# One row maximum bound behind a pair's sums of squares, and one scale per row in the second layer

## The chip, the core and the metric

The kernel runs on one core of a Trainium2 chip. Its engines are PE (TensorE, matrix products), DVE (VectorE), ACT (ScalarE), POOL (GpSimd) and SP (SyncE, which here only issues transfers); each works through its own list of instructions in order and waits for the others by semaphores. The metric is the device time of one execution in microseconds (us). The changed kernel is compared with the kernel before.

## The reference

Three stages, in f32. Four batches of twelve heads (448 tokens, head size 64) go through attention with normalized q and k; the heads are joined to 1792 tokens of 768 columns; two layers with a hidden width of 2048 follow.

```python
q_n, k_n = (rmsnorm(q, g_q), rmsnorm(k, g_k))
scores = scale * np.matmul(q_n, k_n.transpose(0, 1, 3, 2))
attn = np.exp(scores - np.max(scores, axis=-1, keepdims=True))
attn = attn / (np.sum(attn, axis=-1, keepdims=True) + 1e-09)
x = np.matmul(attn, v)            # then joined to 1792 x 768
h = x @ w_in                      # moe: first layer
x = (h * (1.0 / (1.0 + np.exp(-1.702 * h)))) @ w_out
h = x @ w_in                      # moe2: second layer, own weights
out = (np.maximum(h, 0.0) + alpha * np.minimum(h, 0.0)) @ w_out
```

`alpha` has one value for each of the 2048 hidden rows, between 0 and 0.3 in these inputs.

## The kernel before

The matrix products run on pairs of f16 numbers: a value is scaled by a power of two, its high half is rounded to f16 and the rest becomes the low half, and a product is the sum of three matmuls. The powers of two come from maxima: of each row of a weight matrix, of v, of the tokens.

**Order of the work.** The kernel is written as generators that are stepped in turn, but the list of each engine is put in order when the kernel is built: a scheduler with a simulated timeline of its own places every instruction. `tc.issue_after(x)` binds what is issued inside it behind instruction x. So a single binding can move many instructions of all engines, in places that the code does not name.

**The front.** Twenty-four pairs of heads (`P`; six for each batch) are loaded, normalized and put through attention. `normalize` squares a pair's q and k on ACT, and `tensor_reduce` on DVE adds the squares up (`ss`, L423, two for each pair); the inverse root follows on POOL, `qn` (L458) is the normalized product on DVE, PE transposes it (`qt`) and computes scores `sp`. For each unit of scores DVE takes the row maximum `nm` (L530), ACT the exponentials `pr` (L550), PE transposes them (in the first batch) or a DMA does (`pt`), and PE multiplies by v (`xp`, L648). `own` (L666) and `xraw` (L662) finish the first batch's tokens on DVE. A pair's high and low parts `hl` in later batches come from ACT (L477) and DVE (L478).

**The weights of the first layer** are made beside it by `weights`. They arrive as 64-bit words by loads `g` (L223) that SP issues in order, into a few buffers that take turns, so that a load waits until the words before it in its buffer are used up. DVE (L164, L165) and ACT (L148) turn the words into f32; L245 takes each row's maximum `rm`; a few tiny steps (L105, L106, L172) make a power of two of it; ACT and DVE (L180) write the two halves. `w1i` has six blocks of 128 rows and 2048 columns, `w1o` sixteen of 768 columns.

**Two round trips over memory.** A maximum over partitions is found by writing one number per partition to memory and reading the whole line back on every partition. `send_max` does it for `am` (the largest alpha, ready with an L106): L128 writes `line`, L129 reads `row`, and L134 on DVE reduces it into `a`. `measure` does the same for the maxima of v: `vmax` (L106), `v_line` (L329), `vrow` (L330), and `mv` (L331) on DVE.

**The second layer.** `moe2_in` makes tiles `h` (L927; eighteen matmuls each) in three PSUM buffers. ACT copies a tile with the factor `sign` (L932), DVE joins it with the `slope` (L933), and the result `pos` goes to memory. From there `token_sums` reads the tokens back in seven pairs of 128-token tiles: `gp`, or for every second pair `odd`, holds 2 halves of 8 row blocks by 256 tokens. L1029 multiplies it by `cg`, the row's scale from the second weights times the sign of alpha's treatment; then ACT (L1036) and DVE (L1037, L1046 and others) make the seven operands `even` or `odd` of a Strassen-Winograd product, which `moe2_out` multiplies (`op`, L1087). The weights' scales are shared by row block m and m + 8 of the sixteen blocks; `sign` is not. The first two pairs are made while `h` still runs.

Of the kernel before, what the change touches and what calls it, by code (L numbers as in the profile page):

```python
# [13 lines left out]
AF = mybir.ActivationFunctionType  # L14
ALU = mybir.AluOpType
AX = mybir.AxisListType.X
# [41 lines left out]
def attention_moe_kernel(  # L58
# [17 lines left out]
    nc = tc.nc  # L76
# [92 lines left out]
    def row_scales(rm, inv, rows):  # L169

        pow2floor(rm[:, rows], rm[:, rows])
        nc.vector.tensor_scalar(  # L172
            out=inv[:, rows].bitcast(I32), in0=rm[:, rows].bitcast(I32), scalar1=-1.0, scalar2=float((2 * 127 + 13) << 23),
            op0=ALU.mult, op1=ALU.add
        )

    def split_rows(w, num, inv, j):

        nc.scalar.activation(out=w[:, j, 0], in_=num, func=AF.Copy, scale=inv[:, j:j + 1])
        nc.vector.scalar_tensor_tensor(  # L180
            out=w[:, j, 1], in0=num, scalar=inv[:, j:j + 1], in1=w[:, j, 0], op0=ALU.mult, op1=ALU.subtract
        )
# [20 lines left out]
    def weights(src, nm, w, num_tile, raw_tile, parts, ahead, c, done, group, hold=0):  # L203


        rows, cols = src.shape
        words = src.bitcast(I32).rearrange("r (n t) -> r n t", t=2)
        nj = rows // 128
        m = cols // parts
        rm = const.tile([128, nj], F32, name=f"rm_{nm}")  # L210
        inv = const.tile([128, nj], F32, name=f"inv_{nm}")
        raws = []
        nums = []

        def load():
            t = len(raws)
            if t < nj * parts:
                j, i = divmod(t, parts)
                raw = raw_tile(t)
                src_words = words[j * 128:(j + 1) * 128, i * m:(i + 1) * m]  # L220
                if len(raw.shape) == 4:
                    src_words = src_words.rearrange("r (a n) t -> r a n t", a=raw.shape[1])
                loads.setdefault(nm, []).append(nc.sync.dma_start(out=raw, in_=src_words))  # L223
                raws.append(raw)

        def split_all():
            while nums:
                split_rows(w(), nums[0][1], inv, nums[0][0])
                nums.pop(0)
                yield  # L230

        for _ in range(ahead):
            load()
        yield
        for j in range(nj):
            if hold and j == hold:
                yield "held"
                yield from split_all()
            num = num_tile(j)
            for i in range(parts):  # L240
                from_words(num[:, i * m:(i + 1) * m], raws[j * parts + i])
                load()
                yield
            nums.append((j, num))
            nc.vector.tensor_reduce(out=rm[:, j:j + 1], in_=num, op=ALU.max, axis=AX, apply_absolute_value=True)  # L245
            if (j + 1) % group == 0:
                row_scales(rm, inv, slice(j + 1 - group, j + 1))
                yield
                if j >= hold:
                    yield from split_all()  # L250
        if hold:
            yield "rows"
        yield from weight_scales(nm, rm, nj, c, done, W2I_WAIT if hold else 0)
# [8 lines left out]
    w1i = big.tile([128, KD, 2, FF], F16, tag="w", name="w1i", bufs=2)  # L262
# [138 lines left out]
    roots = {}  # L401
    v0 = const.tile([128, NP], F32, name="v0")
    rooted = {}

    def side(P):

        return nc.gpsimd if NP + 2 <= P < 2 * NP else nc.vector

    def normalize(*Ps):
# [4 lines left out]
        n = NT2  # L414
        w = 2 * n * len(Ps)
        ss = small.tile([128, 4 * NT2], F32, tag="ss", name="ss")[:, 0:w]
        for t, P in enumerate(Ps):
            flat = raws[P].rearrange("p h c d -> p (h c) d")
            for i in range(2):
                sq = att_p.tile([128, n, D], F32, tag="sq", name="sq", bufs=SQB)  # L420
                nc.scalar.activation(out=sq, in_=flat[:, i * n:(i + 1) * n], func=AF.Square, scale=2.0 ** -13)
                o = (2 * t + i) * n
                nc.vector.tensor_reduce(out=ss[:, o:o + n], in_=sq, op=ALU.add, axis=AX)  # L423
        nc.gpsimd.tensor_scalar(out=ss, in0=ss, scalar1=1e-6 * 2.0 ** -20, scalar2=None, op0=ALU.add)
        rs = small.tile([128, 4 * NT2], F32, tag="rs", name="rs")[:, 0:w]
        tn = small.tile([128, 4 * NT2], F32, tag="tn", name="tn")[:, 0:w]
# [1 line left out]
            out=rs.bitcast(I32), in0=ss.bitcast(I32), scalar1=-0.5, scalar2=RSQRT_SEED, op0=ALU.mult, op1=ALU.add  # L428
# [421 lines left out]
    KH = KF // 2  # L850
# [26 lines left out]
    w2 = {}  # L877
# [131 lines left out]
    def token_sums(p):  # L1009
# [3 lines left out]
        if p % 2:  # L1013
# [3 lines left out]
            gp = w2["odd"][:, 14336:22528].bitcast(F32)  # L1017
        else:
            ops = big.tile([128, 14336], F16, tag="g", name="even")
            gp = w2["p2"].tile([128, 4096], F32, tag="gp", name="gp", bufs=1)  # L1020
        ops = ops.rearrange("p (o m e t) -> p o m e t", o=7, m=KH, e=2)
        gp = gp.rearrange("p (j m t) -> p j m t", j=2, m=KH)
# [3 lines left out]
        sums[p] = ops  # L1026
        yield
        for m in range(KH):
            nc.scalar.activation(out=gp[:, :, m], in_=gp[:, :, m], func=AF.Copy, scale=w2["cg"][:, m:m + 1])  # L1029
            if m % 4 == 3:  # L1030
                yield
        a11, a12, a21, a22 = (gp[:, j, :, i * 128:(i + 1) * 128] for i in range(2) for j in range(2))
# [273 lines left out]
```

## Time and profile before

| | |
|---|---|
| three timed runs | 1146.89, 1152.3, 1152.42 us (median 1152.3) |
| profiled execution | 1148.87 us, its span 1147.1 us |
| granted clock of TensorE, mean | 0.973 |
| PE busy | 1064.7 us (93% of the span) |
| DVE busy | 802.2 us (70%) |
| ACT busy | 682.2 us (59%) |
| POOL busy | 180.6 us (16%) |

Times of rows are us from the start of the span. "Busy" is the time in which an engine had an instruction running. The bracket behind a row of a timeline is the engine's idle time just before it and what ended that time: `<-DMA row<-line` is the transfer that wrote `row`. Consecutive instructions of one line and shape are put together in a row (x8). An instruction on DVE or ACT starts a little before the last one ends, so a series takes less than the sum of its lengths.

### The profile page before, as it was taken

How to read it: one execution, taken by the hardware profiler on the slowest of the kernel's cores; microseconds unless marked ns; L12 is line 12 of the kernel's file. 1: busy time of each engine (PE TensorE's matmuls, PEld its weight loads, DVE VectorE, ACT ScalarE, POOL GpSimd, SP SyncE). 2: the span in 40 equal slices, each digit the busy share in tenths (PEclk: the TensorE clock that was granted, in tenths of full speed). 3: DMA queues.
4: the chain of work that ended last, by engine and by line, in shares of the span. 5: the costliest groups of instructions: out<-in, count | busy, mean ns of one | idle time of the engine just before them, and what ended most of it. 6: DMA issues, size and time to landing. Idle time of an engine off the chain costs nothing.

```text
span 1147.1 us, 18350 instructions
## 1 busy us (share of the span) xinstructions
PE 1064.7 (93%) x6753; PEld 581.2 (51%) x6753; DVE 802.2 (70%) x1397; ACT 682.2 (59%) x1396; POOL 180.6 (16%) x364
## 2 busy tenths in 40 slices
PE   3787788798989999999999999999999999999998
PEld 1343457644434445555455455444444477666664
DVE  5988798986879885577534965599977223968341
ACT  4788685888879976688633562356455324655220
POOL 2701003676433442100000000000000000000000
PEclk9778899999999999999999999999999999999999
DMA  7964743478888656455346601665342323363111
GB/s 223 271 179 136 175 128 105 97 163 186 176 191 163 163 131 153 110 118 120 78 125 219 214 1 64 246 216 191 143 161 72 136 70 113 101 189 101 34 30 28
DMA packets 235562, 158.19 MB, mean 138 GB/s; under 512 B 167888, under 2 KB 214736, under 8 KB 235472
## 3 DMA queue, kind: packets, MB, share of 16 engines
q1 hardware_dynamic: 229200, 141.34, 44.5%
q0 software_dynamic: 6272, 15.67, 5.2%
q8 instruction: 53, 0.87, 0.3%
q14 instruction: 37, 0.30, 0.1%
HBM read 92.35 MB, written 25.69 MB: 103 GB/s over the span
## 4 chain that ended last, share of the span: by engine, by line
PE 53%; DVE 18%; DMA 12%; issue 7%; ACT 6%; POOL 3%; SPq 1%; ACTq 0%; DVEq 0%; POOLq 0%
PE op L1087 16%; PE yp L821 15%; PE hp L798 7%; PE h L927 7%; PE xp L648 3%; DMA g<-in_moe_w_in_dram 3%; DMA g<-in_moe_w_out_dram 2%; DMA t<-hl 2%; PE sp L525 2%; DVE nm L530 2%; ACT pr L550 2%; DVE g L141 1%; DVE ph L620 1%; DMA yr<-y_dram 1%; DVE pos L933 1%
## 5 line engine op out<-in xcount | busy, mean ns | idle before, releaser
L821 PE MATMUL yp<-g,w1o 128*128 128x448 f16 x1152 | 226.8, 354 | 0.8 <-DVE g L767 0.8
L927 PE MATMUL h<-x,w2i 128*128 128x512 f16 (+1 forms) x1152 | 218.9, 352 | 3.5 <-DVE pos L933 1.9
L798 PE MATMUL hp<-x,w1i 128*128 128x448 f16 x864 | 170.9, 354 | 1.0 <-DVE t L807 1.0
L927 PEld LDWEIGHTS <-w2i 128*128 128x128 f16 x1152 | 112.6, 98 | 109.0 <-issue 4.3
L821 PEld LDWEIGHTS <-w1o 128*128 128x128 f16 x1152 | 109.5, 98 | 110.0 <-issue 11.1
L798 PEld LDWEIGHTS <-w1i 128*128 128x128 f16 x864 | 82.1, 98 | 83.6 <-issue 10.1
L620 DVE SCALAR_TENSOR_TENSOR ph<-pr,sm,ph 128x448 f16<-128x448 f32 x126 | 86.1, 715 | 25.8 <-ACT ph L593 25.8
L530 DVE TENSOR_REDUCE nm<-sp 128x2 f32<-128x896 f32 x96 | 92.6, 964 | 9.5 <-PE sp L525 6.8
L550 ACT ACTIVATE pr<-sp,nm,c_s 128x448 f32<-128x448 f32 x126 | 90.1, 718 | 2.7 <-DVE ph L620 1.4
L932 ACT ACTIVATE pos<-h,sign 128x512 f32<-128x512 f32 (+1 forms) x64 | 40.2, 629 | 86.6 <-PE h L927 75.1
L1087 PEld LDWEIGHTS <-even 128*128 128x128 f16 x672 | 65.7, 98 | 43.4
L933 DVE SCALAR_TENSOR_TENSOR pos<-h,slope,pos 128x512 f32<-128x512 f32 (+1 forms) x64 | 43.5, 681 | 59.4 <-ACT pos L932 59.4
L593 ACT ACTIVATE ph<-pr,sm 128x448 f16<-128x448 f32 x126 | 77.6, 659 | 10.8 <-DVE sm L590 10.7
L758 PE MATMUL hp<-x,w1i 128*128 128x256 f16 (+1 forms) x576 | 61.6, 265 | 13.0 <-DVE g L767 7.6
L1087 PEld LDWEIGHTS <-odd 128*128 128x128 f16 x504 | 49.3, 98 | 32.6
L758 PEld LDWEIGHTS <-w1i 128*128 128x128 f16 x576 | 52.3, 99 | 22.5 <-issue 18.3
L1087 PE MATMUL op<-w2lo,even 128*128 128x384 f16 x384 | 63.4, 326 | 0.0
L648 PE MATMUL xp<-pt,vs 128*64 128x256 f16 (+1 forms) x792 | 49.3, 265 | 9.4 <-DMA pt<-ph 8.3
L525 PE MATMUL sp<-t 64*128 64x448 f16 (+1 forms) x432 | 53.6, 354 | 1.9 <-DMA t<-hl 1.6
L648 PEld LDWEIGHTS <-vs 128*64 128x64 f16 x792 | 37.4, 111 | 29.1 <-issue 17.3
L532 ACT ACTIVATE nm<-nm,c_s 128x2 f32<-128x2 f32 x72 | 20.9, 290 | 49.1 <-DVE nm L530 48.7
L1087 PE MATMUL op<-w2hi,even 128*128 128x384 f16 x288 | 47.5, 326 | 0.0
(243 smaller groups left out, 1649.6 us busy)
## 6 DMA issues: line engine op xcount, KB each, us to landing
g<-in_moe_w_in_dram SPq DMA_DIRECT2D x24, 512.0 KB, 5.9
g<-in_moe_w_out_dram SPq DMA_DIRECT2D x32, 384.0 KB, 4.0
w2raw<-in_moe_w_in_dram SPq DMA_DIRECT2D x24, 512.0 KB, 5.5
w2raw<-in_moe_w_out_dram SPq DMA_DIRECT2D x16, 768.0 KB, 6.4
g_dram<-pos SPq DMA_DIRECT2D x48, 256.0 KB, 2.0
gp<-g_dram SPq DMA_DIRECT2D x8, 1024.0 KB, 6.7
odd<-g_dram SPq DMA_DIRECT2D x6, 1024.0 KB, 5.4
y_dram<-y SPq DMA_DIRECT2D x24, 224.0 KB, 2.5
```

Of the source, the lines that this page charges most:

```text
L525: nc.tensor.matmul(out=sp[:, j, 0:S] if n == 2 else sp[ds, 0, 0:S], lhsT=qt[ds] if n == 2 else qt[ds, 64:128], rhs=kt[ds, 0:S], start=(i = ...
L530: nc.vector.tensor_reduce(out=nm[:, 0:n], in_=sp[:, 0:n, 0:S], op=ALU.max, axis=AX, negate=True)
L550: last = nc.scalar.activation(out=pr[i], in_=sp[:, i, 0:S], func=AF.Exp, bias=nm[:, i:i + 1], scale=c_s if u >= 4 * NP else 1.0, accum_out ...
L593: nc.scalar.activation(out=ph[:, i, 0:S], in_=pr[i], func=AF.Copy, scale=sm[:, i:i + 1])
L620: nc.vector.scalar_tensor_tensor(out=ph[:, i, S:2 * S], in0=pr[i], scalar=sm[:, i:i + 1], in1=ph[:, i, 0:S], op0=ALU.mult, op1=ALU.subtract)
L648: nc.tensor.matmul(out=xp[64 * j:64 * j + 64, t:t + n], lhsT=vs[ks, j, c], rhs=pt[ks, 7 * j + kc, 0:n] if b else pt[ks, kc, o:o + n], star ...
L758: nc.tensor.matmul(out=ps, lhsT=w1i[:, kk, e, m * 128:(m + 1) * 128], rhs=xs[0, kk][:, f, cols], start=(i == 0), stop=(i == 3 * KD - 1))
L798: nc.tensor.matmul(out=ps, lhsT=w1i[:, kk, e, m * 128:(m + 1) * 128], rhs=x[:, f], start=(n == 0), stop=(n == 3 * KD - 1))
L821: nc.tensor.matmul(out=ps, lhsT=w1o[:, m, e, j * 128:(j + 1) * 128], rhs=g[:, m, f], start=(n == 0), stop=(n == 3 * KF - 1))
L927: nc.tensor.matmul(out=ps, lhsT=w2i[:, kk, e, m * 128:(m + 1) * 128], rhs=x2[kk][:, f], start=(c == 0), stop=(c == 3 * KD - 1))
L933: nc.vector.scalar_tensor_tensor(out=pos, in0=ps, scalar=slope[:, m:m + 1], in1=pos, op0=ALU.mult, op1=ALU.max)
L1087: nc.tensor.matmul(out=ps, lhsT=ops[:, o, m, f], rhs=rhs[:, e], start=(c == 0), stop=(c == 3 * KH - 1))
```

## The change

Two places. In `weights` the row maximum of block 0 of `w1i` is bound behind the last `ss` of pair 2, the third pair; the handle of that instruction is kept in `summed`. In `token_sums` one Copy over both halves j, with the scale of block m for both, becomes two Copies, each over one half and with the scale of its own block, j * 8 + m. In these inputs all signs are +1, and both forms compute the same.

```diff
@@ -242,7 +242,9 @@
                 load()
                 yield
             nums.append((j, num))
-            nc.vector.tensor_reduce(out=rm[:, j:j + 1], in_=num, op=ALU.max, axis=AX, apply_absolute_value=True)
+            behind = summed.get(dict(((0, 2),)).get(j)) if nm == "w1i" else None
+            with tc.issue_after(behind.ins) if behind else ExitStack():
+                nc.vector.tensor_reduce(out=rm[:, j:j + 1], in_=num, op=ALU.max, axis=AX, apply_absolute_value=True)
             if (j + 1) % group == 0:
                 row_scales(rm, inv, slice(j + 1 - group, j + 1))
                 yield
@@ -401,6 +403,7 @@
     roots = {}
     v0 = const.tile([128, NP], F32, name="v0")
     rooted = {}
+    summed = {}
 
     def side(P):
 
@@ -420,7 +423,7 @@
                 sq = att_p.tile([128, n, D], F32, tag="sq", name="sq", bufs=SQB)
                 nc.scalar.activation(out=sq, in_=flat[:, i * n:(i + 1) * n], func=AF.Square, scale=2.0 ** -13)
                 o = (2 * t + i) * n
-                nc.vector.tensor_reduce(out=ss[:, o:o + n], in_=sq, op=ALU.add, axis=AX)
+                summed[P] = nc.vector.tensor_reduce(out=ss[:, o:o + n], in_=sq, op=ALU.add, axis=AX)
         nc.gpsimd.tensor_scalar(out=ss, in0=ss, scalar1=1e-6 * 2.0 ** -20, scalar2=None, op0=ALU.add)
         rs = small.tile([128, 4 * NT2], F32, tag="rs", name="rs")[:, 0:w]
         tn = small.tile([128, 4 * NT2], F32, tag="tn", name="tn")[:, 0:w]
@@ -1026,7 +1029,10 @@
         sums[p] = ops
         yield
         for m in range(KH):
-            nc.scalar.activation(out=gp[:, :, m], in_=gp[:, :, m], func=AF.Copy, scale=w2["cg"][:, m:m + 1])
+            for j in range(2):
+                nc.scalar.activation(
+                    out=gp[:, j, m], in_=gp[:, j, m], func=AF.Copy, scale=w2["cg"][:, j * KH + m:j * KH + m + 1]
+                )
             if m % 4 == 3:
                 yield
         a11, a12, a21, a22 = (gp[:, j, :, i * 128:(i + 1) * 128] for i in range(2) for j in range(2))
```

Line numbers of the new kernel lie 2 to 6 higher (L245 is L247 there, L423 L426, L530 L533, L1029 L1033). On DVE the bound maximum stood ahead of an `nm` and the two `ss` of pair 2 and stands behind them. By the second edit alone the lists of PE, DVE, ACT and SP change only in the second layer; the first edit moves instructions of all engines from about 26 us on to the middle of the attention.

On DVE, the stretch from the instruction behind `am` (L106) to `a` (L134) in the kernel before:

```order
L164 TENSOR_SCALAR w1o<-w1o 128x512
L165 SCALAR_TENSOR_TENSOR w1o<-g_144,w1o 128x512 x2
L530 TENSOR_REDUCE nm<-sp 128x2
L180 SCALAR_TENSOR_TENSOR w1i<-w1i,inv_w1i 128x2048
L106 TENSOR_SCALAR rm_w1i<-rm_w1i 128x1
L559 TENSOR_SCALAR sums<-sums 128x4
L165 SCALAR_TENSOR_TENSOR w1o<-g_144,w1o 128x512
L245 TENSOR_REDUCE rm_w1i<-w1o 128x1
L164 TENSOR_SCALAR w1o<-w1o 128x512 x2
L662 TENSOR_TENSOR xraw<-xp,xraw 128x256
L530 TENSOR_REDUCE nm<-sp 128x2
L134 TENSOR_REDUCE a_7327<-row 128x1
```

The same stretch, from behind `am` to `a`, in the new kernel:

```order
L180 SCALAR_TENSOR_TENSOR w1i<-w1i,inv_w1i 128x2048
L164 TENSOR_SCALAR w1o<-w1o 128x512
L165 SCALAR_TENSOR_TENSOR w1o<-g_144,w1o 128x512
L665 TENSOR_TENSOR xraw<-xp,xraw 128x256
L165 SCALAR_TENSOR_TENSOR w1o<-g_144,w1o 128x512
L106 TENSOR_SCALAR rm_w1i<-rm_w1i 128x1
L461 TENSOR_TENSOR qn<-qk,rs 128x2x7x64
L165 SCALAR_TENSOR_TENSOR w1o<-g_144,w1o 128x512
L134 TENSOR_REDUCE a_7327<-row 128x1
```

Two `nm`, a row maximum (L245) and some smaller steps that stood between `am` and `a` now stand elsewhere; `qn` has come in.

On SP, the loads of the weights around the first round trip, before:

```order
L223 DMA g_144<-in_moe_w_in_dram 128x1024 x2
L128 DMA line_7328<-am 128x1
L223 DMA g_144<-in_moe_w_in_dram 128x1024
L129 DMA row<-line_7328 128x128
L223 DMA g_144<-in_moe_w_in_dram 128x1024 x3
L223 DMA g_144<-in_moe_w_out_dram 128x4x192 x12
```

And in the new kernel:

```order
L223 DMA g_144<-in_moe_w_in_dram 128x1024 x3
L128 DMA line_7328<-am 128x1
L129 DMA row<-line_7328 128x128
L223 DMA g_144<-in_moe_w_in_dram 128x1024 x4
L223 DMA g_144<-in_moe_w_out_dram 128x4x192 x14
```

The load that stood between `line` and `row` now stands ahead of `line`.

On ACT, the scaling Copies of the second pair among the evictions `pos`, before:

```order
L1029 ACTIVATE gp<-gp,cg 128x2x256 x2
L932 ACTIVATE pos<-h_9380,sign 128x512
L1029 ACTIVATE gp<-gp,cg 128x2x256 x6
L932 ACTIVATE pos<-h_9403,sign 128x512
L140 ACTIVATE x_9435<-yr,ysc 128x256
```

And in the new kernel, where a Copy has half the elements:

```order
L1033 ACTIVATE gp<-gp,cg 128x256 x8
L935 ACTIVATE pos<-h_9380,sign 128x512
L1033 ACTIVATE gp<-gp,cg 128x256 x8
L935 ACTIVATE pos<-h_9403,sign 128x512
L140 ACTIVATE x_9435<-yr,ysc 128x256
```

A quarter of the pair's Copies stood ahead of the first of the two evictions, and half of them stand there now.

On DVE around the second round trip, `mv` comes after about 4.7 us of other work behind `vmax` in the new list, by the lengths that the same operations have in the trace of before, where it was 8.3; two of the L180 that stood ahead of it stand behind it.

## Rows read from the trace of the kernel before

**Rows 1.** Section 1 of the page: busy us, share of the span, instructions.

```profile
PE 1064.7 (93%) x6753; PEld 581.2 (51%) x6753; DVE 802.2 (70%) x1397; ACT 682.2 (59%) x1396; POOL 180.6 (16%) x364
```

**Rows 2.** Windows: stretch, its length, busy us of each engine, granted clock, DMA share, GB/s.

```profile
60.00:240.00 180.00, 145.28 (x1109) 95.89 (x1106) 158.54 (x338) 136.51 (x314) 42.81 (x70) 0.90 0.52 133
400.00:700.00 300.00, 298.46 (x1918) 152.75 (x1917) 192.23 (x313) 182.67 (x384) 28.12 (x59) 1.00 0.48 128
960.00:1147.10 187.10, 182.35 (x1123) 109.59 (x1120) 106.22 (x149) 70.73 (x100) 0.00 (x0) 1.00 0.28 83
```

**Rows 3.** Timeline of DVE: start, length, engine, line, operation; in brackets idle before, releaser.

```profile
25.80 2.28 DVE L245 TENSOR_REDUCE rm_w1i<-w1i 128x1 f32<-128x2048 f32 x1
```

**Rows 4.** Timeline of DVE, 64 to 84 us, around the first round trip.

```profile
65.31 0.12 DVE L106 TENSOR_SCALAR am<-am 128x1 int32<-128x1 int32 x1
...
65.69 1.28 DVE L165 SCALAR_TENSOR_TENSOR w1o<-g,w1o 128x512 int32<-128x512 int32 x2
...
67.95 2.34 DVE L180 SCALAR_TENSOR_TENSOR w1i<-w1i,inv_w1i 128x2048 f16<-128x2048 f32 x1
...
77.59 0.29 DVE L134 TENSOR_REDUCE a<-row 128x1 f32<-128x128 f32 x1 [1.81 <-DMA row<-line]
...
81.27 0.43 DVE L164 TENSOR_SCALAR g<-g 128x512 int32<-128x512 int32 x1 [2.78 <-ACT g L148]
```

**Rows 5.** Timeline of SP's queue, 60 to 140 us: start, length of the issue.

```profile
65.46 0.33 SPq L128 DMA_DIRECT2D line<-am  x1
66.43 0.33 SPq L223 DMA_DIRECT2D g<-in_moe_w_in_dram  x1
73.54 0.33 SPq L129 DMA_DIRECT2D row<-line  x1
...
126.91 0.50 SPq L329 DMA_DIRECT2D v_line<-vmax  x1
...
131.88 0.34 SPq L330 DMA_DIRECT2D vrow<-v_line  x1
```

**Rows 6.** Timeline of DVE, 100 to 213 us: pauses that the argument goes through.

```profile
103.81 1.09 DVE L530 TENSOR_REDUCE nm<-sp 128x2 f32<-128x896 f32 x1 [2.64 <-PE sp L516]
...
126.42 0.16 DVE L106 TENSOR_SCALAR vmax<-vmax 128x2 int32<-128x2 int32 x1
...
136.35 0.42 DVE L331 TENSOR_REDUCE mv<-vrow 128x2 f32<-128x256 f32 x1 [1.51 <-DMA vrow<-v_line]
...
142.38 0.42 DVE L666 SCALAR_TENSOR_TENSOR own<-xp,first_sc,own 128x192 f32<-128x192 f32 x1 [3.30 <-PE xp L648]
...
209.93 1.09 DVE L478 TENSOR_TENSOR hl<-qk,hl 128x896 f16<-128x896 f32 x1 [2.31 <-ACT hl L477]
```

**Rows 7.** Section 5 of the page: busy, mean ns, idle before, releaser.

```profile
L648 PE MATMUL xp<-pt,vs 128*64 128x256 f16 (+1 forms) x792 | 49.3, 265 | 9.4 <-DMA pt<-ph 8.3
```

**Rows 8.** Timeline of ACT, second layer.

```profile
865.75 5.01 ACT L1029 ACTIVATE gp<-gp,cg 128x512 f32<-128x512 f32 x8 [4.22 <-DVE cg L1160]
...
894.75 1.34 ACT L1029 ACTIVATE gp<-gp,cg 128x512 f32<-128x512 f32 x2 [6.98 <-DMA gp<-g_dram]
...
900.80 1.30 ACT L140 ACTIVATE x<-yr,ysc 128x256 f16<-128x256 f32 x3
...
970.01 2.94 ACT L1036 ACTIVATE odd<-odd 128x1024 f16<-128x1024 f32 x3
```

**Rows 9.** Timeline of PE, second layer.

```profile
858.91 17.43 PE L927 MATMUL h<-x,w2i 128*128 128x512 f16 x80
...
894.70 2.28 PE L1087 MATMUL op<-w2lo,even 128*128 128x384 f16 x13
897.49 4.69 PE L927 MATMUL h<-x,w2i 128*128 128x512 f16 x21 [0.51 <-DVE pos L933]
...
978.38 15.76 PE L1087 MATMUL op<-w2lo,odd 128*128 128x384 f16 x96
```

**Rows 10.** Timeline of DVE, second layer: its half of an eviction.

```profile
871.40 0.75 DVE L933 SCALAR_TENSOR_TENSOR pos<-h,slope,pos 128x512 f32<-128x512 f32 x1
```

## Prediction

> **What bounds the kernel now.** I read the busy shares first, then windows over the stages, then DVE's rows with the idle time ahead of each, then SP's, PE's and ACT's at the places that DVE's pauses named. The profiled execution took 1148.87 us, 1147.1 of it the span; the three timed runs lie from 1146.89 to 1152.42. PE is busy 93% of the span [rows 1], and what it lacks it lacks in front: over 60:240 it is busy 145.28 of 180 us and DVE 158.54, over 400:700 PE has 298.46 of 300 [rows 2]. In front DVE has the least room of all engines, each of its pauses has a name, and a pause that grows moves everything behind it, PE's matmuls included. At the end matmuls stand back to back. So the time is PE's work, which the change leaves as it is, plus PE's pauses: those that DVE hands down in front, and some at the second layer's first pairs.
>
> **The change, part by part.** It has two edits with separate places. The bound row maximum (L245, 2.28 us at 25.80 [rows 3]) stands some 2 us later on DVE, behind nm and the two ss that came right after it. No work is added or removed, and by about the 440th DVE instruction the same set stands in front of both orders: DVE work has only traded places with DVE work, and the direct price is nothing. What counts is that the order of all engines changes up to about 600 us, so that DVE's pauses meet other neighbours. I go through them by name.
>
> *The first round trip over memory* (am to a). am is ready at 65.31 + 0.12 = 65.43; its line is issued at 65.46, landed 8 us later, the broadcast row issued at 73.54, and a starts at 77.59 after a wait of 1.81 [rows 4, 5]. Between am and a DVE now has 10.35 us of work (65.43 to 77.59 less 1.81). In the new order there stand L180 2.34, L164 0.43, three L165 of 0.64 (half of a pair of 1.28), xraw and a small one, 0.5 together, and qn, 1.1 as nm on as many elements [rows 4, 6]: 6.3, less 0.07 for each of seven starts ahead of the end before it, or about 5.8 us. Besides, on SP the load issued at 66.43, between line and row, comes ahead of the line. At 66.43 it went out just after the first L165 behind am had ended (65.69 + 0.64 = 66.33). In the new order that L165 ends 3.2 us behind am (L180, L164, itself). From that load to a it is 77.59 - 66.43 = 11.2 us, so a is ready 14.4 us behind am and DVE waits 14.4 - 5.8 = 8.6 instead of 1.81: **+6.8**. Queued behind it are the integer steps that feed the weights and, five rows on, nm, for which ACT's exponentials wait. Two pauses pay it back. The g of L164 at 81.27 waited 2.78 for a load that SP holds behind the row [rows 4]; it stands about 4 us further from a in the new order, so it is covered: **-2.8**. And nm at 103.81 waited 2.64 for PE's scores [rows 6]; ACT and PE catch up while DVE stands, and 1.6 us more DVE work lies ahead of it: **-2.6**. Bounds: the trip covered by work I don't see, -1.8, against +6.8 with nothing given back. I take the sum of the three, +1.4, since each has its own row.
>
> *The second round trip* (vmax to mv). vmax ends at 126.58, v_line is issued at 126.91, vrow at 131.88, mv starts at 136.35 after 1.51 of waiting [rows 5, 6]: 9.77 us from end to start, with 8.3 of DVE work in it. In the new order 4.7 us of work stand there (two L180 are now behind mv), so the wait grows to about 5.0: **+3.5**. Behind it own waited 3.30 for xp [rows 6]; own now stands 6.0 us of work behind mv instead of 2.5, so that pause goes: **-3.3**. Together +0.2, bounds -4.8 and +3.5.
>
> Here the Trainium skill speaks against me: "DMA: Bandwidth & Descriptors", section "Latency and other measured facts", puts the access to HBM at 0.2 us on average and 2 at high load, and calls that the dominant part of a fixed cost of about 2 us per DMA. By it two hops would be an estimated 4 us, less than either stretch of work, and both waits would go. The trace does not agree: the hops took 8.0 and 4.0, 5.0 and 4.5 us [rows 5, 6], and I hold to the trace.
>
> *The first high and low parts* (hl, 2.31 <-ACT at 209.93 [rows 6]): in the new order one us less of DVE work lies between the two of them: **+1.0**, bounds -2.3 and +1.0.
>
> *Waits of PE for transposes.* All through the attention PE waits 8.3 us for pt, the transposed weights that come by DMA [rows 7], four times between 280 and 370. The order of that stretch changes too, but I see neither which of them stays nor a new one; 0, bounds -8.3 and +8.3.
>
> *The sign.* In the second layer 56 Copies of 128x512 (eight in 5.01 us, 0.626 from start to start [rows 8]) become 112 of 128x256. The trace has no such Copy from f32 to f32; the nearest are L140's three on 128x256 in 1.30 us, 0.40 from start to start (three starts and a last end of 0.1 more [rows 8]). By that sixteen take 6.4, **1.4 us more a pair**; bounds 0 (half the width at half the price) and +5.0 (the full 0.626 each). Over seven pairs it is 10 us of ACT, which from 960 on has 70.73 of 187.1 busy [rows 2]: what matters is who waits. For the odd operand of 978.38, the third Copy of L1036 ends at 970.01 + 2.94 = 972.95 [rows 8, 9]: 5.4 us to spare. So only the first two pairs count, whose Copies stand among the evictions of h.
> - First pair: the eviction at 870.66 stands behind the eight Copies; DVE's half of it ends 871.40 + 0.75 = 872.15 [rows 10]. PE has three buffers for h and 18 matmuls a tile (six chunks by three products) of 0.218 us each (17.43 over 80 [rows 9]); counted from 858.91, with eight left of the tile before, it asks for that buffer at 858.91 + 62 x 0.218 = 872.4. So 0.3 of the 1.4 is hidden, **+1.1**.
> - Second pair: PE already waits 0.51 at 897.49 [rows 9] for an eviction, ahead of which two Copies of this pair stand (1.34 [rows 8]). In the new order eight half Copies stand there, 3.3 us, 2.0 more; five more matmuls of op (18 for 13, 0.17 each from 2.28 over 13 [rows 9]) are in front of PE: 2.0 - 0.9 = **+1.1**.
>
> Sum: front 1.4 + 0.2 + 1.0 = 2.6, sign 2.2: **+4.8** on 1148.87, **1153.7**, say 1154. Against the median of the three runs, 1152.3, that is 0.2% more; counted from the median it would be 1157, and my range takes that in. A difference under 0.5% (5.8 us) is about what a measurement of this kernel can't tell from none.
>
> **Rivals.**
> - *The new order feeds the pairs earlier* (faster). The third pair's normalized product stands 3.8 us of DVE work earlier, the fourth's 6.3. For it: PE waits for such products in the whole stretch of [rows 2]. Then g 2.78, nm 2.64 and own 3.30 go, half of the 8.3 of pt goes with them, and the two trips wait no longer than now: -12.9 + 1.0 + 2.2 = -9.7, **1139**. Against it: less work stands behind both trips. The skill's rule on the fixed cost, if it held in the new surroundings, would make this the likelier case.
> - *Both trips are paid in full* (slower). One mechanism, DVE in order behind a broadcast that comes back over memory, at 66 to 78 and 126 to 136. If PE and ACT live from hand to mouth on DVE, nothing catches up while it stands, and the paybacks only turn up elsewhere: 6.8 + 3.5 + 1.0 + 2.2 = +13.5, **1162**. It decides where a is ready over about 12 us behind am and DVE has under 6 us of work there. For it: PE's and DVE's pauses in 60:240 go together. Against it: three of the pauses have releasers other than DVE [rows 4, 6].
> - *The half Copies cost as much as whole ones* (slower). Sixteen take 10.0: the first pair loses 5.0 - 0.3 = 4.7, the second eight times 0.626 less 1.34 less 0.9 = 2.8, with the front's 2.6 +10.1, **1159**. Against it: L140's 0.40.
> - *The bind does nothing that counts*: the front gives 0, the sign 2.2, **1151**. This lies inside my forecast.
>
> **How the numbers follow.** The forecast with the last rival 0.40 (own range 1147 to 1157, all within 5.8 us of what before does); pairs earlier 0.32; trips in full 0.20; whole-price Copies 0.08. That makes faster 0.32, same 0.40, slower 0.28. The range reaches into the first rival to 1140 and past the slower ones' middle to 1164, which leaves out about 0.1 at either end.
>
> **What would show it.** Right: a of L134 waits 8 to 9 us behind row and mv near 5 behind vrow, while the pauses of g, nm and own are gone; DVE's and PE's sums over 20:260 within 3 us of now; Copies on 128x256 near 0.50 us each; PE waits of about 1 us for pos near 872 and of 1.6 near 897. Wrong: a or mv without a wait (first rival); PE in 60:240 losing 10 us (second); sixteen Copies in 10 us (third); or a stall past 250 of which nothing is said above, above all another set of waits for pt.

## The result, and the profile after

The new kernel takes 1160.92 us in the median of 7 runs (1157.16 to 1161.52), the kernel before 1152.3 (7 runs, 1145.62 to 1155.93): ratio 1.0091, 95% interval 1.0068 to 1.0114 (the two medians alone would make 1.0075, inside it). It is slower by some 8 to 13 us. The forecast was 1154, no difference, with 0.28 for slower; the time lies inside the range, in the part that the range kept for the slower rivals. The profiled execution took 1157.16 us, its span 1155.4, 8.3 us more than that of before.

Where do the 8.3 us arise? The first and the last start of a line on PE are milestones. These are the rows of one line each, in the kernel before: the second product of the first layer (`yp`) and the first product of the second layer (`h`). Behind the count stand the shortest, median and longest duration in ns.

```profile
L821 PE MATMUL yp<-g,w1o x1152: 349/352/581, 235.0 to 728.6; 128*128 128x448 f16 x192
...
L927 PE MATMUL h<-x,w2i x1152: 272/379/379, 728.8 to 956.0; 128*128 128x512 f16 x144, 128*128 128x256 f16 x48
```

The same two in the kernel after (L824 and L930):

```profile
L824 PE MATMUL yp<-g,w1o x1152: 349/352/363, 240.8 to 736.9; 128*128 128x448 f16 x192
...
L930 PE MATMUL h<-x,w2i x1152: 272/379/379, 737.1 to 965.3; 128*128 128x512 f16 x144, 128*128 128x256 f16 x48
```

The first `yp` starts at 240.8 for 235.0: 5.8 us are lost by then. The first `h` starts at 737.1 for 728.8: 2.5 more are lost in between. That is one execution of each kernel; the experiments show below how far such marks scatter. From the first `h` to the end it is 418.3 us in both (1147.1 - 728.8, 1155.4 - 737.1): the second layer, where the sign is, takes nothing more.

The window of after over the front, to set beside [rows 2]:

```profile
60.00:240.00 180.00, 144.79 (x1114) 97.81 (x1111) 153.57 (x329) 132.32 (x309) 40.55 (x67) 0.88 0.47 129
```

DVE is busy 153.57 us of 60:240 instead of 158.54, so its pauses have grown by 5.0, and PE's work there is the same within 0.5 (144.79 for 145.28, at a mean granted clock of 0.88 for 0.90, between its two levels in both). This is DVE around the two round trips in the kernel after, for [rows 4] and [rows 6]:

```profile
77.60 0.29 DVE L134 TENSOR_REDUCE a<-row 128x1 f32<-128x128 f32 x1 [6.47 <-DMA row<-line]
...
95.83 0.17 DVE L562 TENSOR_SCALAR sums<-sums 128x4 f32<-128x4 f32 x1 [1.19 <-ACT pr L553]
...
110.59 1.08 DVE L533 TENSOR_REDUCE nm<-sp 128x2 f32<-128x896 f32 x1
...
143.25 0.42 DVE L333 TENSOR_REDUCE mv<-vrow 128x2 f32<-128x256 f32 x1 [2.48 <-DMA vrow<-v_line]
...
149.56 0.40 DVE L669 SCALAR_TENSOR_TENSOR own<-xp,first_sc,own 128x192 f32<-128x192 f32 x1
```

And SP's queue:

```profile
59.88 4.06 SPq L223 DMA_DIRECT2D g<-in_moe_w_in_dram  x3
65.36 0.33 SPq L128 DMA_DIRECT2D line<-am  x1
73.66 0.33 SPq L129 DMA_DIRECT2D row<-line  x1
74.09 7.84 SPq L223 DMA_DIRECT2D g<-in_moe_w_in_dram  x4
...
135.81 0.34 SPq L331 DMA_DIRECT2D v_line<-vmax  x1
138.94 0.34 SPq L332 DMA_DIRECT2D vrow<-v_line  x1
```

a is reached 6.47 us before row has landed (1.81 before). The line goes out right behind am, at 65.36, as it did in [rows 5]. The section on the change has one thing wrong here: the load that stood between line and row has not moved ahead of line. The three loads ahead of line are loads that stood ahead of it before; the list shows only how many stand in a row. The load of 66.43 now stands behind row, as the first of four where there were three, and SP issues it at 74.09. The g of 81.27 no longer waits, and mv waits 2.48 (1.51 before). The nm that waited 2.64 at 103.81 runs at 110.59 and the own that waited 3.30 at 142.38 runs at 149.56, both without a bracket: neither waits. A new pause of 1.19 stands at sums (95.83). So the pauses named around the two trips did what was said, in sign. What was not foreseen are the pauses that came in their place. Who waited for whom on DVE between 140 and 240 us, before:

```profile
DVE own L666 <- PE xp L648: 4.1, 2, 3.3
DVE hl L478 <- ACT hl L477: 2.3, 1, 2.3
DVE num1o L164 <- ACT num1o L148: 2.1, 1, 2.1
DVE g L767 <- DMA g<-in_moe_w_out_dram: 0.7, 2, 0.5
DVE qk L444 <- POOL rs L434: 0.5, 1, 0.5
```

And after:

```profile
DVE g L770 <- ACT t L769: 2.7, 3, 1.3
DVE w1o L164 <- ACT w1o L148: 2.6, 5, 1.4
DVE mv L333 <- DMA vrow<-v_line: 2.5, 1, 2.5
DVE qk L447 <- POOL rs L437: 1.7, 1, 1.7
DVE own L669 <- PE xp L651: 1.3, 2, 0.7
...
DVE nm L533 <- PE sp L528: 1.0, 1, 1.0
```

own, hl and num1o gave back 2.8, 2.0 and 2.1 us, and g, w1o (L164), mv, qk and nm took 2.0 (2.7 for 0.7), 2.6, 2.5, 1.2 and 1.0 (the 1.51 at mv in before fell just ahead of 140). Not all of this belongs to the order: in three other kernels with before's lists in front (experiments 1, 4 and 7) hl waits only 1.1 to 1.8 and num1o 0.8 or 0.9, and w1o (L164) 1.6 to 2.0. Three waits set the two orders apart in every profile. The own named above waits 1.8 to 3.3 us in the eight kernels with before's lists from 92 us on (before and experiments 1, 4, 7, 8, 9, 11, 12), and not at all in the six with the bound ones (after, 2, 3, 5, 6, 10). qk waits 0.5 in the eight and 1.7 in the six, and the g that waits for ACT's t at most 0.4 and 2.1 to 4.1 (over 92:246). Over the front the pauses of DVE are 6.7 us in 20:100, 6.6 in 100:140 and 9.7 in 140:240 before, and 11.4, 4.0 and 13.8 after (the stretch less DVE's busy time).

### The profile page after: what moved, and what is told of

Read it like the earlier page. It is cut to its first block, busy times and chain, and to the rows that moved or that the text cites. A ratio compares the mean times of both kernels' runs of the same rounds, so it can differ in the third digit from the quotient of the medians.

```text
span 1155.4 us, 18407 instructions
## 1 busy us (share of the span) xinstructions
PE 1070.2 (93%) x6753; PEld 585.0 (51%) x6753; DVE 801.2 (69%) x1397; ACT 690.4 (60%) x1452; POOL 181.4 (16%) x364
## 4 chain that ended last, share of the span: by engine, by line
PE 57%; DVE 14%; DMA 12%; issue 6%; ACT 6%; POOL 4%; SPq 1%; DVEq 0%; ACTq 0%; POOLq 0%
PE op L1093 17%; PE yp L824 13%; PE hp L801 11%; PE h L930 9%; PE xp L651 3%; PE sp L528 2%; DMA qk<-in_q_dram 2%; DMA g<-in_moe_w_in_dram 2%; ACT pr L553 1%; DMA yr<-y_dram 1%; DVE ph L623 1%; DMA pt<-ph 1%; DMA w2raw<-in_moe_w_in_dram 1%; DMA w2raw<-in_moe_w_out_dram 1%; DVE w2num L165 1%
## 5 line engine op out<-in xcount | busy, mean ns | idle before, releaser
L824 PE MATMUL yp<-g,w1o 128*128 128x448 f16 x1152 | 225.8, 353 | 2.0 <-ACT g L140 0.9
L930 PE MATMUL h<-x,w2i 128*128 128x512 f16 (+1 forms) x1152 | 219.3, 352 | 3.4 <-DVE pos L936 2.5
L930 PEld LDWEIGHTS <-w2i 128*128 128x128 f16 x1152 | 112.6, 98 | 108.7 <-issue 4.2
L824 PEld LDWEIGHTS <-w1o 128*128 128x128 f16 x1152 | 109.5, 98 | 110.4 <-issue 11.2
L533 DVE TENSOR_REDUCE nm<-sp 128x2 f32<-128x896 f32 x96 | 92.6, 965 | 5.8 <-PE sp L528 5.1
L761 PE MATMUL hp<-x,w1i 128*128 128x256 f16 (+1 forms) x576 | 64.1, 272 | 14.3 <-DVE g L770 5.2
L651 PE MATMUL xp<-pt,vs 128*64 128x256 f16 (+1 forms) x792 | 49.6, 265 | 11.2 <-DMA pt<-ph 10.9
```

Source lines behind the costliest of these rows:

```text
L533: nc.vector.tensor_reduce(out=nm[:, 0:n], in_=sp[:, 0:n, 0:S], op=ALU.max, axis=AX, negate=True)
L651: nc.tensor.matmul(out=xp[64 * j:64 * j + 64, t:t + n], lhsT=vs[ks, j, c], rhs=pt[ks, 7 * j + kc, 0:n] if b else pt[ks, kc, o:o + n], star ...
L761: nc.tensor.matmul(out=ps, lhsT=w1i[:, kk, e, m * 128:(m + 1) * 128], rhs=xs[0, kk][:, f, cols], start=(i == 0), stop=(i == 3 * KD - 1))
L824: nc.tensor.matmul(out=ps, lhsT=w1o[:, m, e, j * 128:(j + 1) * 128], rhs=g[:, m, f], start=(n == 0), stop=(n == 3 * KF - 1))
L930: nc.tensor.matmul(out=ps, lhsT=w2i[:, kk, e, m * 128:(m + 1) * 128], rhs=x2[kk][:, f], start=(c == 0), stop=(c == 3 * KD - 1))
```

## The experiments

For the parts of the order to be told apart, the lists of the engines had to be held fixed, since any edit lets the scheduler place everything anew. Each instruction has a name that is the same in the kernel before and in the bound one. So from the third experiment on the kernel is the kernel before, with the order of each engine, up to where the two orders are the same again, written out as a table of names and bound link by link:

```diff
+ORDER = {
+    "PE": ("..."),
+    "DVE": ("..."),
...
+}
+def follow(tc, nc):
+    traced = {i.name: i for i in nc.cur_bb.bb.instructions}
+    how = mybir.DependencyInfo(mybir.DependencyClass.NoSync, mybir.DependencyReason.DATA)
+    for told in ORDER.values():
...
+        for one, nxt in zip(names, names[1:]):
+            tc.add_manual_dep(traced[nxt], one, how, reason="order")
...
         attention_moe_kernel(tc, *args)
+        follow(tc, nc)
```

With the bound kernel's own order in the table this gives the bound kernel's lists on all five engines; with a cut, everything that the one kernel issues ahead of an instruction stands in its order, and the rest in the order of the other. Each ratio is to runs of the kernel before in the same 5 rounds on the same chip. Their median was 1149.75 us for experiments 1 to 4, 1150.89 for 5 to 8 and 1151.14 for 9 to 12, which ran on another chip, and a ratio is not quite the quotient of two medians; so equal medians can stand beside different ratios.

| | order | median us | ratio | 95% interval | PE's first yp / first h against before's |
|---|---|---|---|---|---|
| 1 | sign alone | 1150.33 | 1.0019 | 0.9996 to 1.0042 | +2.9 / +5.0 |
| 2 | bind alone | 1161.79 | 1.0106 | 1.0082 to 1.0130 | +11.7 / +12.9 |
| 3 | bound to 246 us, then before | 1160.68 | 1.0105 | 1.0077 to 1.0133 | +4.0 / +7.8 |
| 4 | before to 240 us, then bound | 1155.59 | 1.0036 | 1.0014 to 1.0058 | -1.6 / +7.9 |
| 5 | bound, a later | 1160.63 | 1.0075 | 1.0044 to 1.0107 | +8.2 / +10.6 |
| 6 | bound, row and a later | 1157.40 | 1.0054 | 1.0033 to 1.0075 | +7.1 / +13.1 |
| 7 | before, row and a later | 1149.38 | 0.9996 | 0.9972 to 1.0020 | -2.3 / -1.8 |
| 8 | bound to 92 us, then before | 1157.06 | 1.0062 | 1.0035 to 1.0088 | +5.2 / +5.9 |
| 9 | as 8, row and a later | 1154.92 | 1.0024 | 0.9994 to 1.0055 | +5.1 / +7.1 |
| 10 | before to 92, bound to 246, before | 1158.33 | 1.0066 | 1.0044 to 1.0089 | +4.5 / +11.3 |
| 11 | before, 4.6 us more on DVE | 1161.11 | 1.0101 | 1.0070 to 1.0132 | +5.2 / +10.4 |
| 12 | before, 9.2 us more on DVE | 1171.34 | 1.0179 | 1.0154 to 1.0205 | +10.3 / +20.9 |

The last column is of one profiled execution each, and those scatter: the first, whose front has before's order, is 2.9 us late at the first yp. The second has the new kernel's lists up to the second layer and is 11.7 late there, where the new kernel was 5.8. The profiled execution of the sixth is its slowest, 1160.87. So what counts are the ratios; the column only says roughly where.

The wait of a can be read in eight of these profiles and in those of the two kernels. With the bound order up to there it is 6.47 (the new kernel), 7.40 (2), 8.62 (3) and 8.39 (8), with before's 1.81 (before), 2.94 (1), 2.89 (4), 3.90 (10), 3.44 (11) and 2.83 (12): 7.7 and 3.0 in the mean. The longest:

```profile
79.05 0.29 DVE L134 TENSOR_REDUCE a<-row 128x1 f32<-128x128 f32 x1 [8.62 <-DMA row<-line]
```

The way from am to a takes as long in both orders, 12.3 to 14.4 us and 12.2 to 13.7. What differs is the work that DVE has in it, 5.8 us for 10.35, and that is nearly all of the 4.7 by which the wait grows.

**1, the sign alone.**

```diff
-            nc.scalar.activation(out=gp[:, :, m], in_=gp[:, :, m], func=AF.Copy, scale=w2["cg"][:, m:m + 1])
+            for j in range(2):
+                nc.scalar.activation(
+                    out=gp[:, j, m], in_=gp[:, j, m], func=AF.Copy, scale=w2["cg"][:, j * KH + m:j * KH + m + 1]
+                )
```

> The kernel before with the second edit alone (one Copy for each row block, 112 of 128x256). The two profiles say that the second layer costs nothing: from the first matmul of h to the end it is 418.3 us in both. Theory A (all of the loss comes from the bind): within 2 us of before. Theory B (the prediction's +2.2 at the first two pairs is there, but the new front hides it): +2 us or more. Copies on 128x256 at about 0.50 us each by both.

1.0019, 0.9996 to 1.0042: between nothing and 5 us, and with theory A as with B's +2. The profile of after decides what the Copies do. On ACT:

```profile
873.31 6.49 ACT L1033 ACTIVATE gp<-gp,cg 128x256 f32<-128x256 f32 x16 [4.06 <-DVE cg L1166]
879.71 0.66 ACT L935 ACTIVATE pos<-h,sign 128x512 f32<-128x512 f32 x1
...
901.61 3.30 ACT L1033 ACTIVATE gp<-gp,cg 128x256 f32<-128x256 f32 x8 [4.75 <-DMA gp<-g_dram]
```

And on PE:

```profile
866.63 13.54 PE L930 MATMUL h<-x,w2i 128*128 128x512 f16 x62
881.24 4.04 PE L930 MATMUL h<-x,w2i 128*128 128x512 f16 x18 [1.06 <-DVE pos L936]
...
903.80 3.09 PE L1093 MATMUL op<-w2lo,even 128*128 128x384 f16 x18
906.73 5.56 PE L930 MATMUL h<-x,w2i 128*128 128x512 f16 x25
```

Sixteen half Copies take 6.49 us, 1.48 more than the eight, and PE waits 1.06 for pos at 881.24. Both are the terms of the prediction (+1.4, +1.1). At the second pair, though, the wait of 0.51 at 897.49 in [rows 9] is gone. The pair's data had come by 901.61, 2.2 us ahead of the block of op at 903.80; in before the first Copies began with that block (894.75 [rows 8], 894.70 [rows 9]). So in this execution the sign costs 1.06 - 0.51, half a microsecond. In the profile of the first experiment the waits are 0.50 at the first pair and none at the second, and the sign costs nothing; the 1.1 of the prediction depends on how PE stands when the Copies begin.

**2, the bind alone.**

```diff
+            behind = summed.get(dict(((0, 2),)).get(j)) if nm == "w1i" else None
+            with tc.issue_after(behind.ins) if behind else ExitStack():
```

> The kernel before with the first edit alone. Theory A: the whole loss, +7 to +10 us against before, ratio near 1.008. Theory B: +5 to +7, the rest being the sign's.

1.0106: the whole loss, theory A (12 us, a little above its +7 to +10). What follows is about the order that this binding makes.

**3 and 4, its front and its back.** The table holds the bound kernel's order up to the instruction that it runs on DVE at 246 us, and before's for all that is left; and the other way round, with the cut at 240 us of before.

```diff
+# 3: bound[:cut at 246 us] + [i for i in before if not in it]
+# 4: before[:cut at 240 us] + [i for i in bound if not in it]
```

> The kernel before with the order of every engine written out: that of the bound kernel for what it issues up to about 246 us, that of before for the rest. Theory A1 (the front loses 6 us of DVE pauses, the later attention 2.5 us more of waits for pt): +5 to +7. Theory A2 (PE's slack behind the front swallows what DVE lost, and the order of the later attention alone makes the loss): within 3 us of before.

> The mirror: the order of before up to about 240 us, that of the bound kernel behind it. Theory A1: +2 to +3.5. Theory A2: +7 or more.

The front alone costs 1.05%, twice what A1 allowed for; the back alone 0.36%, +4 us, in A1's way. A2 falls. Together they make 1.41%, for 1.06 with both: 0.35 too much, within the 0.43 that the three intervals leave. What the back loses shows in PE's waits for the transposed weights, here the fourth experiment's row, to set beside [rows 7]:

```profile
L648 PE MATMUL xp<-pt,vs 128*64 128x256 f16 (+1 forms) x792 | 49.5, 264 | 14.8 <-DMA pt<-ph 14.7
```

14.7 us instead of 8.3. It is one execution; with the same lists behind 246 us the second, fifth and sixth have 9.6, 10.3 and 13.9. In the kernel after it is 10.9:

```profile
L651 PE MATMUL xp<-pt,vs 128*64 128x256 f16 (+1 forms) x792 | 49.6, 265 | 11.2 <-DMA pt<-ph 10.9
```

**5 and 6, the round trip of am in the bound order.** The fifth moves two instructions on DVE; the sixth one more, on SP.

```diff
 DVE
-a <- row (L134)
 w1o, rm, inv, w1o, sums
-ra <- a
...
 nm (L530, at about 96 us)
+a <- row
+ra <- a
 SP, the sixth alone
 line <- am
-row <- line
 g <- in_moe_w_in x4
+row <- line
 g <- in_moe_w_out
```

> The order of the bound kernel, written out, with one move on DVE: the reduce that makes a from row, and its reciprocal, stand 35 instructions later (behind the nm that ran at about 96 us), so that DVE doesn't stand 6.47 us for row. Nothing else moves; SP still waits for line ahead of four weight loads. Theory C (the wait at a costs what it lasts beyond before's, 4.7 us): 4 to 6 us faster than the bound kernel, within 0.5% of before. Theory D (the loads that SP holds behind row end the wait, not a): the pause moves to the g of L164 or L165 and 0 to 2 us come back.

> As the last, and on SP row is issued behind the four loads of the first weights that it held back. Theory C: no more than the last. Theory D: now 4 to 6 us come back, 1154 to 1157 beside a before of 1150. If neither gives anything back, what DVE lost at a is lost again behind it (ACT's exponentials, the loads of v), and the front's loss has another place.

1.0075 and 1.0054, for 1.0106 with the trip in place. The sixth is better than the bound order by 0.52% (the two intervals make this 0.2 to 0.8), about 6 us; the fifth lies between and is told apart from neither. In the fifth the pause moves, as theory D said. DVE, pauses that begin in 70:90:

```profile
74.41 0.43 DVE L164 TENSOR_SCALAR w1o<-w1o 128x512 int32<-128x512 int32 x1 [1.36 <-ACT w1o L148]
76.13 0.17 DVE L559 TENSOR_SCALAR sums<-sums 128x4 f32<-128x4 f32 x1 [1.29 <-ACT pr L550]
...
80.36 0.43 DVE L164 TENSOR_SCALAR g<-g 128x512 int32<-128x512 int32 x1 [3.46 <-ACT g L148]
```

In the sixth, with the loads ahead of row:

```profile
76.38 0.43 DVE L164 TENSOR_SCALAR w1o<-w1o 128x512 int32<-128x512 int32 x1 [2.15 <-ACT w1o L148]
78.09 0.17 DVE L559 TENSOR_SCALAR sums<-sums 128x4 f32<-128x4 f32 x1 [1.29 <-ACT pr L550]
...
79.87 0.43 DVE L164 TENSOR_SCALAR g<-g 128x512 int32<-128x512 int32 x1 [1.00 <-ACT g L148]
```

Its SP no longer stands: the loads go out from 69.12 on and row behind them.

```profile
69.12 10.14 SPq L223 DMA_DIRECT2D g<-in_moe_w_in_dram  x4
79.32 0.42 SPq L129 DMA_DIRECT2D row<-line  x1
```

The pauses at these places come to 6.1 us in the fifth and 4.4 in the sixth, where the new kernel had 6.47 at a. So the trip holds both queues: DVE by a, and SP, with the weights behind row. By the times it is worth about half of the loss. The profile of the sixth, its slowest execution, doesn't show the gain: DVE's pauses over 20:260 come to 31.5 us, for 30.7 in the new kernel and 34.6 in the second. The other half stays.

**7, the same move in the order of before.** The edit of the sixth, in before's lists (a and ra 24 instructions later, behind an nm; row behind three loads).

```diff
 SP
-row <- line
 g <- in_moe_w_in x3
+row <- line
```

> The order of before, written out, with the same two moves: row behind the loads that it held back, a and its reciprocal 24 instructions later. DVE waited 1.81 at a and 2.78 at the g behind it. Theory D: 2 to 4.6 us faster than before. If pauses of the front are given back by those behind, no difference.

0.9996, 0.9972 to 1.0020: no gain that can be told, and none above some 3 us. (It also shows that writing the order out costs nothing by itself.) Most of the 1.81 and 2.78 of [rows 4] comes back as other waits in the same place:

```profile
74.47 0.43 DVE L164 TENSOR_SCALAR w1o<-w1o 128x512 int32<-128x512 int32 x1 [1.12 <-ACT w1o L148]
...
78.49 0.43 DVE L164 TENSOR_SCALAR g<-g 128x512 int32<-128x512 int32 x1 [2.12 <-ACT g L148]
79.96 0.43 DVE L164 TENSOR_SCALAR g<-g 128x512 int32<-128x512 int32 x1 [1.04 <-ACT g L148]
...
80.91 1.09 DVE L530 TENSOR_REDUCE nm<-sp 128x2 f32<-128x896 f32 x1 [0.46 <-PE sp L516]
```

That is 4.7 us, for 5.1 in before (1.81, 2.78 and 0.5 at w1o). With 10 us of work behind it the trip costs nothing that can be told, with 5.8 it costs.

**8, 9 and 10, the front in parts.** Bound order to 92 us, past a and its wait; the same with the move of the sixth; and the bound order only from 92 to 246 us.

```diff
+# 8: bound[:cut at 92 us] + rest of before
+# 9: the same, with row behind four loads, a and ra behind the nm at 96 us
+# 10: before[:cut at 92 us] + bound[:cut at 246 us] + rest of before
```

> The order of the bound kernel up to about 92 us, past a and its wait, and the order of before from there on. Theory C or D: the loss at a is kept, +3 to +5 against before. Rival: the front's loss arises later, about mv (126 to 160 us) and the first weights' end: within 2 us of before.

> The order of the bound kernel up to about 92 us, of before from there on, and the two moves of the sixth experiment (row behind the four loads, a and its reciprocal behind the nm at about 96 us). Without the moves this order was 0.6% slower than before. Theory C/D (that loss is the round trip of am): within 0.25% of before. Rival (the other work that the bind moves in front, the later row scales and products, costs as much as the trip): 0.4 to 0.6% slower still.

> The order of before up to about 92 us, of the bound kernel up to about 246, of before from there on. If the parts add up, this is what is left of the front: 1.05% less 0.6%, or +4 to +5 us. If the middle loses only because DVE comes late into it, +0 to +1.

The stretch with the trip costs 0.62%, 7 us where 3 to 5 were expected, and 0.24% with the trip moved (0.9994 to 1.0055); the difference, 0.38%, is as large as its own uncertainty (0.4), so the ninth agrees with the sixth and doesn't settle it alone. The stretch behind, 92 to 246 us, costs 0.66% by itself, more than the +4 to +5 expected: it is no mere echo of the trip, which isn't in it. Who waited for whom on DVE between 140 and 240 us, in the tenth:

```profile
DVE g L767 <- ACT t L766: 2.8, 4, 1.1
...
DVE qk L444 <- POOL rs L434: 1.7, 1, 1.7
```

These are the new kernel's waits (2.7 and 1.7), here behind a trip of am in before's order. The eighth, with the trip in the bound order and before's order behind it, has at most 0.4 and 0.5 there. So these pauses belong to the order from 92 us on and aren't handed down by a. In the tenth's profile the waits for pt are nearly as large as in the fourth:

```profile
L648 PE MATMUL xp<-pt,vs 128*64 128x256 f16 (+1 forms) x792 | 50.7, 270 | 14.0 <-DMA pt<-ph 14.0
```

**11 and 12, DVE time added by itself.** Two or four reduces over 128x2048 elements of a constant, into a new tile that nothing reads, behind the g that waits until 81.27 in [rows 4].

```diff
         second_layer(late)
+        spare = const.tile([128, 16], F32, name="spare")
+        for _ in range(2):    # 12: range(4)
+            nc.vector.tensor_reduce(
+                out=spare, in_=identf.unsqueeze(1).to_broadcast([128, 16, 128]), op=ALU.max, axis=AX
+            )
```

> The order of before, written out, and two reduces more on DVE (each over 128x2048 elements, about 2.3 us, their result unused) right behind the g that waited until 81.27, ahead of a nm. Theory P (in front DVE's time passes through to the end whole): +4 to +5 us. Rival Q (the pauses behind it, nm 2.64 and own 3.30, swallow it): within 1.5 us of before.

> The same with four such reduces, about 9 us. Theory P: +8 to +10. Rival Q: the first 4 to 6 us are swallowed, the rest passes: +3 to +5.

They take 4.60 us of DVE and 9.24. The eleventh:

```profile
81.53 4.60 DVE L1278 TENSOR_REDUCE spare<-identf 128x16 f32<-128x2048 f32 x2
...
108.15 1.09 DVE L530 TENSOR_REDUCE nm<-sp 128x2 f32<-128x896 f32 x1 [2.55 <-PE sp L516]
...
146.88 0.42 DVE L666 SCALAR_TENSOR_TENSOR own<-xp,first_sc,own 128x192 f32<-128x192 f32 x1 [3.31 <-PE xp L648]
```

1.0101 and 1.0179: +10 and +20 us by the medians, twice what theory P had and far more than Q's. The milestones split it. At the first yp PE is 5.2 and 10.3 us late: up to there DVE's time passes whole, as P says, in one execution each, and the pauses of nm (2.55) and own (3.31) are still there: Q falls. By the first h they are 10.4 and 20.9 us late. That other half shows in the waits for pt, 4.0 us more than before's in the eleventh:

```profile
L648 PE MATMUL xp<-pt,vs 128*64 128x256 f16 (+1 forms) x792 | 49.5, 265 | 12.3 <-DMA pt<-ph 12.3
```

But this half isn't clean. In the views of DMA issues (issuer, count, median us to landing) the transposes themselves are slower, all through the kernel. Before:

```profile
pt<-ph SPq DMA_TRANSPOSE x90, 3.6
```

The eleventh:

```profile
pt<-ph SPq DMA_TRANSPOSE x90, 4.1
```

The twelfth has 4.1 too, and every other kernel of this study 3.6 or 3.7. The new tile has 64 bytes per partition, and all buffers that come behind it lie 64 bytes further on. No run separates the later start from the slower transfers, or the shifted buffers from the added DVE time, which both kernels have.

## Why the prediction was right or wrong

- *The number.* The sum had +4.8 over the profiled execution of before, and +8.3 was measured. The time lies inside the range by the room that the range kept for the slower rivals, not by the sum.
- *The place.* Right: the loss is the bind's, not the sign's, and in front time added on DVE passes to PE whole (11 and 12, up to the first yp).
- *The round trip of am.* The wait grew from 1.81 to 6.47, foretold 8.6. The step that put a load ahead of line is wrong, since that load stands behind row; without it the same working gives 12.2 - 5.8 = 6.4. Other executions of the same order had 7.40 to 8.62, so the 8.6 by itself is not refuted, but before's 1.81 was the shortest of six: the growth is 4.7 also in the mean, for +6.8 in the sum. That it is paid for is shown by the sixth experiment (about 6 us back).
- *What pays it back.* This step failed. The pauses of g (2.78), nm (2.64) and own (3.30) did go, as the sum had it (the row of g names ACT; that the load is behind it, as the prediction reads it, fits ACT's own wait of 1.62 for g at 80.57). But I counted pauses that go and none that come: in 140:240 DVE lost 13.8 us instead of 9.7, at g, w1o, qk and nm, none of which had a row to be named from. The eighth and tenth experiments show that those of g and qk come with the order behind 92 us, with or without the trip. By the milestone the front cost 5.8 in this execution, foretold 2.6.
- *The second round trip.* mv grew by 1.0 instead of 3.5, since the trip itself got shorter: 7.5 us from vmax to mv instead of 9.8, with 5.0 us of work in it. It is 7.3 to 8.0 in all six kernels with the bound order there and 9.7 to 10.6 in the eight with before's. The prediction took its length over from before. In before SP issued two loads between v_line and vrow, and it issues none there now; that these are the reason is not shown.

```profile
127.51 0.92 SPq L223 DMA_DIRECT2D g<-in_moe_w_out_dram  x2
```

- *hl.* Foretold +1.0; it gave back 2.0 (2.3 to 0.3), of which about half is before's own scatter (1.1 to 1.8 in experiments 1, 4 and 7).
- *The waits for pt.* Set to 0 with bounds of 8.3 either way. They grew by 2.6 (8.3 to 10.9), as much as the 2.5 us between the first yp and the first h. The term was inside its bounds and on the slower side. Its size isn't settled: with before's lists behind 246 us six profiles have 6.8 to 9.5 and the tenth 14.0 (11 and 12, with their slower transfers, left aside), with the bound ones five have 9.6 to 14.7.
- *The sign.* The Copies as worked out (+1.48 a pair for +1.4). The first wait is 1.06 for 1.1 here and 0.50 in the first experiment, so its agreement is partly luck. The second wait went to 0 instead of growing by 1.1: I let the pair's Copies begin with the block of op, as in before, and they began 2.2 us ahead of it. +0.5 for +2.2.
- *The rivals.* Both trips in full gave 1162, and 1161 was measured, but not for its reason: the second trip cost 1.0, the paybacks took place, and its sign, PE losing 10 us in 60:240, is missing (0.5). Of the forecast's own signs PE's sum over 20:260 held (1.1 us less) and DVE's did not (209.35 for 214.03, 4.7 less where 3 were allowed). The first half of that rival, DVE in order behind what comes back over memory, is shown for the first trip alone. The faster rival (pairs fed earlier) has nothing for it in any run.
- *The length of a hop.* The Trainium skill, "DMA: Bandwidth & Descriptors", section "Latency and other measured facts", has about 2 us as the fixed cost of a DMA. The hops of line and row took 8.3 and 3.9 us here (65.36, 73.66, 77.60), and those of v_line and vrow 3.1 and 4.3 (135.81, 138.94, 143.25). This trace doesn't agree either, and the waits were there.

What stays open: the bound order from 92 to 246 us costs 0.66% without the trip (10), and the waits at g and qk come with it, but no run took one of them away to show what it is worth; the second trip, which lies in that stretch, was not moved in any. And it is open what of the pt waits follows from a later start and what from which transpose stands next to which load.

## What to carry to other kernels

When an edit lets a scheduler place everything anew, a sum over the pauses that go is half a sum: set against it what the same engine lost per window in total, and give the range a slower lean if work has been taken out from behind a wait that comes back over memory. Count the work behind such a wait and the transfers queued behind its issue, since both are held. To learn what an order costs, write the order out and change one link; a re-scheduled kernel answers another question. And read a wait in more than one execution before building on it: the wait of a had 1.8 to 3.9 us in one and the same order.

## What the runs showed that was not expected

- With one unused tile of 64 bytes per partition in the middle of the memory, the 90 transposes of pt landed in 4.1 us in the median instead of 3.6, in both kernels that had it and in no other. Both also had the added reduces, so the cause is not isolated.
- 4.6 us of DVE at 82 us cost 10 us at the end, and 9.2 cost 20; half of each in front, half in the attention behind it.
- One and the same order gave a wait of 1.8 to 3.9 us at a in six kernels, and 6.5 to 8.6 in four with the other.
